# A planner's table of durations and hand-over times is replaced, and the first pair's product is placed behind the scores of all four first pairs

## The chip, the cores and the metric

The kernel runs on one core of one Trainium2 chip. The metric is the device time of one launch in microseconds (us). The core has five instruction streams that run side by side and wait for each other by semaphores: TensorE (PE), VectorE (DVE), ScalarE (ACT), GpSimd (POOL) and SyncE (SP), from which nearly all DMAs are issued.

## The reference

Windowed attention over 8 batches and 8 heads (576 tokens, 64 wide) is followed by a gated MLP over all 4608 tokens. Four heads see the last 32 positions, four see every fourth of the last 128.

```python
scores = scale * np.matmul(q, k.transpose(0, 1, 3, 2))
scores = np.where(masks[None, :, :, :], scores, -1000000000.0)
scores = scores - np.max(scores, axis=-1, keepdims=True)
attn = np.exp(scores)
attn = attn / (np.sum(attn, axis=-1, keepdims=True) + 1e-09)
out = np.matmul(attn, v)                       # (8, 8, 576, 64)
x = out.transpose(0, 2, 1, 3).reshape(4608, 512)
h = x @ w_in                                   # 512 -> 2048
g = h * (1.0 / (1.0 + np.exp(-1.702 * h)))
result = g @ w_out                             # 2048 -> 512
```

## The kernel before

Each f32 operand of the MLP is held as a high part, rounded to the matmul's input format, and a low part, the remainder, and a product is three matmuls (high by high, low by high, high by low).

**Attention** is made for pairs of heads. There are 32 pairs, four for each batch; pair k has number k % 4 in batch k // 4. A pair's scores (`scores`, L463) go to the PSUM tile `sp`. The softmax (`softmax`, L514) takes the row maximum (L502), subtracts it (L349), exponentiates on ACT (L506), sums (L520), adds 1e-9 to the sum (L510), inverts it (L512), and multiplies twice, once for each head (L349, on POOL or DVE). Then the weights are transposed by 32 x 32 blocks into `ct` (L529 for the first batch, L533 else). The first batch (pairs 0 to 3) is done by `first_attention` (L682) and `first_product` (L559), which writes the PSUM tile `first_x`. `drain_x` (L612) copies it on ACT into `xs` as the high part, and DVE subtracts to get the low part, also in `xs`; the last 64 tokens go to a rest. The four pairs give the four channels (128 rows each) of the first batch's tokens.

**The MLP** runs for batch 0, 1 and 2 as a `Group` (L817): for each of 16 units f, 12 large matmuls make `hp_m` (L848), ACT makes a tanh (L856), DVE the gating (L857), ACT and DVE split the result into `gh` and `gl`, and 12 more large matmuls add to `acc_m` (L785, L786, L789). Unit 1 of the first group uses the bank `sp`, unit 2 the bank `av`, all others the one bank `hp`. The batches after that run as three `Block`s of two with a scheme of seven products in place of eight (`up_p`, `up_q`, `up_r` at L991, `second_*` at L1106).

**Weights** come as f64 bit patterns and are decoded on the chip by `decode` (L355): n even is a `w_in` unit, n odd a `w_out` unit. A decode is a DMA (L384), two word operations on ACT (L394, L395), the sign on ACT (L388) or DVE (L390), a shift on DVE (L398), two pair operations on DVE, one of which POOL can take (L349), and a copy to the high part on ACT or DVE (L342, L344). They run during the first group, each ahead of the unit that needs it.

**The order.** The kernel does not write its order by hand. Every piece of work is given to `Plan.add` (L58) with its costs by engine (a negative cost on DVE marks one that shares a port with POOL), an urgency, a function that issues it, and the names it reads and writes. `Plan.placed` (L111) then runs a model of the five engines: it puts each piece on the engine where it would end first, in the order of the modelled times, taking the most urgent of those that can start. `LATENCY` (L45) is the model's time between the end of a piece and the start of a piece on another engine that needs it. `fetched` (L134) models that PE's instructions arrive in pieces of 256, with edges at 193 + 256 j. Where PE would be idle early on, `ordered` puts in filler matmuls: large ones (`idle<-ident`) or small ones (`idle<-ones`). After 130 us of the model's time it is redone three times with due times (`latest`, L80). The engines then run their lists strictly in this order. So a changed number can move any instruction of the program.

## Time and profile before

| | |
|---|---|
| median of 3 runs | 829.24 us (827.79 to 829.8) |
| the profiled execution's own time | 828.89 us |
| span of its trace | 827.2 us |
| mean granted clock of PE | 0.991 |
| HBM read and written | 140.64 and 45.09 MB |
| DMA, mean over the span | 227 GB/s |

The span is the time from the first to the last instruction in the trace; the rest of the execution's own time lies around it. In the profile, PE is the matmuls and PEld the weight loads that overlap them. A row such as `PE hp_m L848 <- DVE xs L349: 0.4, 1, 0.4` says that PE waited before line 848, which writes `hp_m`, 0.4 us in total, once, 0.4 us at the longest, for DVE's line 349 writing `xs`; where nothing in the profile released an engine, "issue" stands there. In a timeline, a row has the start, the busy time, engine, line, operation, output and inputs, and how many instructions it merges. A large matmul's busy time, about 0.39 us, overlaps the next one's.

### The profile page before, as it was taken

What the parts mean: (1) busy time and instruction counts of PE and PEld (TensorE: products, weight loads), DVE (VectorE), ACT (ScalarE), POOL (GpSimd) and SP (SyncE); (2) the same over time, 40 slices, a digit from 0 to 9 for tenths busy, and PEclk for the clock granted to TensorE, in tenths of its full rate; (3) what the DMA queues carried; (4) which work ended last, traced back from release to release, by engine and by line L of the source; (5) the groups of instructions that cost most, each with busy time, mean ns of one, the idle gap of its engine ahead of it and who ended that gap; (6) DMA issues with size and microseconds to landing.
All of it is one profiled execution on the core that took longest, in us unless ns stands there. A gap on an engine that the chain in (4) does not pass through costs nothing.

```text
span 827.2 us, 18837 instructions
## 1 busy us (share of the span) xinstructions
PE 811.2 (98%) x7240; PEld 653.5 (79%) x7240; DVE 669.7 (81%) x1104; ACT 515.0 (62%) x992; POOL 327.8 (40%) x296
## 2 busy tenths in 40 slices
PE   7899999999999999999999999999999999999997
PEld 4678777888878888878788788888888888888886
DVE  6898989787888778898989998977679876867575
ACT  7998986676676777586776655446446544544340
POOL 3343336566655663324235357331125431112251
PEclk8799999999999999999999999999999999999999
DMA  9476658889757567868878878675665658664546
GB/s 359 152 244 193 181 192 287 295 281 314 249 189 254 183 200 257 267 190 280 279 229 261 261 233 260 219 269 168 214 193 182 211 186 273 203 222 149 189 151 181
DMA packets 109610, 188.12 MB, mean 227 GB/s; under 512 B 26448, under 2 KB 55376, under 8 KB 109520
## 3 DMA queue, kind: packets, MB, share of 16 engines
q1 hardware_dynamic: 109376, 186.78, 69.3%
q8 instruction: 57, 0.93, 0.5%
q14 instruction: 33, 0.27, 0.1%
q10 hardware_dynamic: 144, 0.13, 0.0%
HBM read 140.64 MB, written 45.09 MB: 225 GB/s over the span
## 4 chain that ended last, share of the span: by engine, by line
PE 88%; DVE 7%; ACT 1%; issue 1%; DMA 1%; SPq 0%; DVEq 0%; ACTq 0%
PE hp_m L848 15%; PE up_q L991 9%; PE up_r L991 9%; PE up_p L991 8%; PE second_q_Q L1106 5%; PE second_r_Q L1106 5%; PE second_p_Q L1106 5%; PE acc_m L785 5%; PE acc_m L789 5%; PE acc_m L786 4%; PE sp L482 3%; PE second_r_Z L1106 3%; PE second_R L1106 3%; PE second_q_Z L1106 3%; PE second_p_Z L1106 2%; PE av L607 2%
## 5 line engine op out<-in xcount | busy, mean ns | idle before, releaser
L349 POOL TENSOR_TENSOR arena<-arena 128x256 f32<-128x256 f32 (+3 forms) x109 | 118.0, 1091 | 155.7 <-DVE wi_last_units L349 34.7
L848 PE MATMUL hp_m<-xs,wi_kept 128*128 128x512 f32 x504 | 129.1, 398 | 0.7 <-DVE xs L349 0.4
L848 PEld LDWEIGHTS hp_m<-xs,wi_kept 128*128 128x128 f32 x504 | 93.3, 188 | 22.5 <-DVE arena L857 1.6
L342 ACT ACTIVATE wo_kept<-arena 128x512 fp32r<-128x512 f32 x115 | 71.9, 629 | 42.3 <-PE second_r_Q L1106 11.4
L349 POOL TENSOR_TENSOR wo_kept<-arena,wo_kept 128x512 fp32r<-128x512 f32 x34 | 45.3, 1340 | 105.5 <-ACT wo_kept L342 72.2
L991 PE MATMUL up_p<-wi_kept,xs 128*128 128x512 f32 x336 | 84.7, 394 | 2.2 <-DVE arena L349 1.3
L991 PE MATMUL up_r<-wi_kept,xs 128*128 128x512 f32 x336 | 85.3, 389 | 0.0
L991 PE MATMUL up_q<-wi_kept,xs 128*128 128x512 f32 x336 | 83.4, 389 | 0.0
L991 PEld LDWEIGHTS up_p<-wi_kept,xs 128*128 128x128 f32 x336 | 62.1, 188 | 16.8 <-DVE arena L349 2.2
L991 PEld LDWEIGHTS up_q<-wi_kept,xs 128*128 128x128 f32 x336 | 63.0, 188 | 13.4 <-DVE arena L1013 0.3
L991 PEld LDWEIGHTS up_r<-wi_kept,xs 128*128 128x128 f32 x336 | 63.1, 188 | 13.1
L349 DVE TENSOR_TENSOR wo_kept<-arena,wo_kept 128x512 fp32r<-128x512 f32 x87 | 65.3, 761 | 5.9 <-ACT wo_kept L342 5.4
L349 POOL TENSOR_TENSOR wo_kept<-wi_last_units,wo_kept 128x512 fp32r<-128x512 f32 x23 | 31.9, 1388 | 84.6 <-ACT wo_kept L342 84.6
L785 PE MATMUL acc_m<-gh,wo_kept 128*128 128x512 f32 x156 | 61.7, 395 | 0.4 <-ACT arena L342 0.3
L786 PE MATMUL acc_m<-gh,wo_kept 128*128 128x512 f32 x156 | 60.9, 390 | 0.0
L349 POOL TENSOR_TENSOR pr<-pr,sm 128x320 f32<-128x320 f32 x52 | 43.3, 850 | 43.0 <-DVE sm L512 29.3
L342 ACT ACTIVATE bt<-ct 32x256 f32<-32x256 f32 (+1 forms) x127 | 55.2, 435 | 3.2 <-DVE ct L533 0.9
L1012 ACT ACTIVATE arena<-arena 128x512 f32<-128x512 f32 x60 | 37.5, 628 | 28.9 <-DVE arena L349 25.1
L349 DVE TENSOR_TENSOR gl<-arena,gh 128x512 fp32r<-128x512 f32 x53 | 44.9, 847 | 9.1 <-PE acc_m L789 6.4
L349 DVE TENSOR_TENSOR arena<-arena 128x512 f32<-128x512 f32 (+1 forms) x68 | 50.4, 747 | 0.4
L1013 DVE SCALAR_TENSOR_TENSOR arena<-arena 128x512 f32<-128x512 f32 x60 | 48.1, 807 | 0.7 <-ACT arena L1012 0.2
L342 ACT ACTIVATE wo_kept<-wi_last_units 128x512 fp32r<-128x512 f32 x47 | 29.6, 629 | 30.0 <-PE second_r_Z L1106 8.9
(261 smaller groups left out, 1826.6 us busy)
## 6 DMA issues: line engine op xcount, KB each, us to landing
xs<-sums SPq DMA_DIRECT2D x168, 256.0 KB, 3.3
out_weights<-sums_o SPq DMA_DIRECT2D x63, 512.0 KB, 3.8
qk<-qk_dram SPq DMA_DIRECT2D x29, 576.0 KB, 5.2
xs<-sums_o SPq DMA_DIRECT2D x21, 512.0 KB, 3.6
v<-vp_dram SPq DMA_DIRECT2D x28, 320.0 KB, 4.4
sums<-arena SPq DMA_DIRECT2D x32, 256.0 KB, 3.6
sums_o<-arena SPq DMA_DIRECT2D x32, 256.0 KB, 3.4
arena<-wi_dram SPq DMA_DIRECT2D x15, 512.0 KB, 4.7
```

The lines of the kernel that those rows point to most:

```text
L342: A.activation(dst, src, AF.Copy, scale=scale)
L349: (V if e == DVE else G).tensor_tensor(out=dst, in0=a, in1=b, op=op)
L482: T.matmul(dst[:, w:w + n], u["qk"][rows, at:at + 32], u["qk"][rows, S + first:S + first + n], start=not masked(k), stop=True, tile_positi ...
L607: T.matmul(u["x"][i][rows, at:at + last - first], u["v"][keys, a, m], bt[keys, m, a, first:last], start=(bank_, a) not in begun, stop=True ...
L785: T.matmul(self.acc[j], w[:, 0, cols], high, start=f == 0, stop=False)
L786: T.matmul(self.acc[j], w[:, 1, cols], high, start=False, stop=False)
L789: T.matmul(self.acc[j], w[:, 0, P * j:P * j + P], low, start=False, stop=f == NF - 1)
L848: T.matmul(hps[f], wi(f)[:, st, cols], mv[:, c], start=c == 0 and k == 0, stop=c == NC - 1 and k == 2)
L991: T.matmul(self.banks[place], xs[:, slot, at:at + P], wi_kept[:, 2 * a + c, mv], start=fresh and c == 0 and k == 0, stop=c == 1 and k == 2 ...
L1012: add({ACT: 0.60}, -10.0, lambda e: A.activation(unit(tmp), src(), AF.Tanh, scale=0.851), need, own(tmp))
L1013: add({DVE: -0.70 if need[0][0] == "A" else 0.70}, -10.0, lambda e: V.scalar_tensor_tensor(out=unit(dst), in0=unit(tmp), scalar=1.0, in1=s ...
L1106: T.matmul(self.second[key], w[:, st, cols], mv, start=fresh and y == 0 and k == 0, stop=y == 1 and k == 2, skip_group_check=True)
```

## The change

It has five parts.

1. **Hand-over times.** `LATENCY` goes from 0.2 or 0.3 us to 0.04 to 0.09 for the compute engines. A new table `FROM` keeps 0.2 and 0.3 for some ways (from PE, and after a DMA). `LEAVES` lets the model's engine take its next piece 0.045 to 0.10 us before the last one ends.
2. **Durations.** Several costs are changed, and an early instruction piece is taken to arrive 4.2 us after the edge before it where that edge is crossed before 6 us.
3. **The 1e-9** may be added on ACT.
4. **The first product.** `first_attention` no longer makes the product. It is made by the new `first_multiplied`, which reads a name that the fourth pair's scores write; the transposes, split off as `first_transposed`, stand ahead of it for pairs 0 and 1 and behind the product of the pair two ahead for pairs 2 and 3. Each product writes a name of its own (`four`), which `drain_x` reads.
5. **Zeros.** The zeroing of `bt` on POOL has urgency 44 in place of 20.

```diff
-LATENCY = {PE: 0.3, ACT: 0.2, DVE: 0.2, POOL: 0.2, DMA: 0.2}
+LATENCY = {PE: 0.06, ACT: 0.04, DVE: 0.04, POOL: 0.09, DMA: 0.2}
+FROM = {PE: {ACT: 0.2, DVE: 0.2}, DMA: {PE: 0.3, ACT: 0.2, DVE: 0.2, POOL: 0.2}}
+LEAVES = {PE: 0.0, ACT: 0.10, DVE: 0.085, POOL: 0.045, DMA: 0.0}
...
-                blocks.append(at + (6.1 if at < 18.0 else 4.2))
+                blocks.append(at + (4.2 if at < 6.0 else 6.1 if at < 18.0 else 4.2))
...
+            leaves = when + cost - min(LEAVES[e], 0.6 * cost)
             if e == POOL or (e == DVE and ops[i][0][e] < 0):
-                port[0] = when + cost
-
-            free[e] = when + (cost if e != DMA else 0.7 if cost < 100 else 0.43)
+                port[0] = leaves
+
+            free[e] = leaves if e != DMA else when + (0.7 if cost < 100 else 0.43)
...
-                    gap = 0.0 if to == e == PE else 0.13 if to == e else LATENCY[to]
+                    gap = 0.0 if to == e == PE else FROM.get(e, {}).get(to, LATENCY[to])
...
-        add({DVE: -0.75, ACT: 1.37}, urgency, take_sign, (R,), (R + "l",))
+        add({DVE: -0.65, ACT: 1.22}, urgency, take_sign, (R,), (R + "l",))
...
-        add({DVE: -0.15}, urgency, lambda e: V.tensor_scalar(
-            out=sm, in0=sm, scalar1=1.0e-9, scalar2=None, op0=ALU.add), (), (SM,))
+        def shift(e):
+            if e == ACT:
+                A.activation(sm, sm, AF.Copy, bias=1.0e-9)
+            else:
+                V.tensor_scalar(out=sm, in0=sm, scalar1=1.0e-9, scalar2=None, op0=ALU.add)
+
+        add({ACT: 0.2, DVE: -0.15}, urgency, shift, (), (SM,))
...
-            add({POOL: 0.85, DVE: -0.48}, urgency, lambda e, a=a: pair(
+            add({POOL: 0.73, DVE: -0.48}, urgency, lambda e, a=a: pair(
...
-            costs = {DMA: 82} if k < FIRST * NC else {ACT: 0.49, DVE: -0.33}
+            costs = {DMA: 82} if k < FIRST * NC else {ACT: 0.45, DVE: -0.29}
...
+            four = f"four{turn(k)}"
...
-                    e, part(xh[:, c]), src()), FOUR, (f"xh{c}.{n}",))
+                    e, part(xh[:, c]), src()), (four, *FOUR), (f"xh{c}.{n}",))
...
-    def first_attention(k, urgency):
+    def first_attention(k):
+
 
         load_qk(k)
         load_v(k)
-        add({PE: 1.5 if k else 2.3}, urgency - 1.0e5, lambda e: scores(k), (lots(k)[0],), ("sp",), count=180)
-        softmax(k, urgency)
-        add({PE: 1.4}, urgency - 1.0e5, lambda e: first_product(k), (lots(k)[1], f"ct{turn(k)}.0", f"ct{turn(k)}.1"), FOUR,
-            count=184)
-        drain_x(k, urgency)
+        add({PE: 1.5 if k else 2.3}, k - 1.0e5, lambda e: scores(k), (lots(k)[0],), ("sp", f"scores{k}"), count=180)
+        softmax(k, k)
+
+    def first_transposed(k):
+        y = turn(k)
+        pr, ct = prs[y], cts[y].rearrange("p h t a q -> p (h t a q)").rearrange("p (a n) -> p a n", a=2)
+        for a in range(2):
+            add({DVE: 0.50}, k, lambda e, a=a: V.transpose(
+                out=ct[:, a, 0:QT * W], in_=pr[:, a].rearrange("p t w -> p (t w)")), (f"pr{y}", f"pr{y}.{a}"), (f"ct{y}.{a}",))
+
+    def first_multiplied(k):
+
+
+        y = turn(k)
+        add({PE: 1.4}, k - 1.0e5, lambda e: first_product(k), (lots(k)[1], f"ct{y}.0", f"ct{y}.1", f"scores{NC - 1}"),
+            (f"four{y}",), count=184)
+        drain_x(k, k)
...
     for c in range(NC):
-        first_attention(c, c)
+        first_attention(c)
+        if c < 2:
+            first_transposed(c)
         if c in (1, 2):
             decode(c - 1, c + 1.3)
+    for c in range(NC):
+        first_multiplied(c)
+        if c < 2:
+            first_transposed(c + 2)
...
-            add({POOL: 1.2}, 20.0, lambda e: G.memset(bt, 0.0), (), ("bt", "btl", *zeroed))
+            add({POOL: 1.2}, 44.0, lambda e: G.memset(bt, 0.0), (), ("bt", "btl", *zeroed))
```

Lines in the changed kernel are shifted by up to 24. What the change does to the order is seen at three places.

On PE, right behind the first pair's scores (`sp_187`), there stood seven large fillers before; the first rows are:

```order
L482 MATMUL sp_187<-qk_126 32x64 x3
L482 MATMUL sp_187<-qk_126 32x48
L482 MATMUL sp_187<-qk_126 32x16
L1237 LDWEIGHTS ident
L1237 MATMUL idle<-ident 128x512
```

and now 19 small ones, behind which the second pair's scores (`sp_262`) begin:

```order
L487 MATMUL sp_187<-qk_126 32x64 x3
L487 MATMUL sp_187<-qk_126 32x48
L487 MATMUL sp_187<-qk_126 32x16
L1265 MATMUL idle<-ones 32x16 x19
L475 LDWEIGHTS ident
L475 MATMUL sp_262<-plain,ident 128x320
```

The seven large fillers are gone from there. Of the 30 large fillers of the program 13 are left, eight ahead of the third pair's scores and five ahead of the fourth's.

On PE, the fourth pair's scores (`sp_439`) were followed by the second pair's product and the first large matmuls of unit 0:

```order
L482 MATMUL sp_439<-arena 32x64 x3
L482 MATMUL sp_439<-arena 32x48
L482 MATMUL sp_439<-arena 32x16
L575 MATMUL first_x<-ct_92,arena 64x32 x6
L575 MATMUL first_x<-ct_92,arena 64x64 x24
L575 MATMUL first_x<-ct_92,arena 64x48 x8
L575 MATMUL first_x<-ct_92,arena 64x16 x8
L848 MATMUL hp_m_0_556<-xs,wi_kept 128x512 x3
```

Now (`sp_401`) the first pair's product stands there, and the other three come behind it:

```order
L487 MATMUL sp_401<-arena 32x64 x3
L487 MATMUL sp_401<-arena 32x48
L487 MATMUL sp_401<-arena 32x16
L580 MATMUL first_x<-ct_91,v_129 64x32 x6
L580 MATMUL first_x<-ct_91,v_129 64x64 x24
L580 MATMUL first_x<-ct_91,v_129 64x48 x8
L580 MATMUL first_x<-ct_91,v_129 64x16 x8
L580 MATMUL first_x<-ct_92,arena 64x32 x6
```

The first pair's product has moved from behind the third scores to behind the fourth. The large matmuls have moved from among the products to behind the last of the four, with no filler between: nine of unit 0 (channels 0 to 2), three of unit 1, three of unit 0 (channel 3), nine of unit 1, six of unit 2, and then the first `acc_m`.

On ACT, from the tanh of unit 0 to that of unit 1, stood these rows (L394, L395 and L388 are decode's word operations and sign, L342 copies to a high part):

```order
L856 ACTIVATE arena<-hp_m_0_556 128x512
L394 ACTIVATE arena<-arena 128x512
L395 ACTIVATE arena<-arena 128x512
L342 ACTIVATE wi_kept<-arena 128x512
L342 ACTIVATE gh_73<-arena 128x512
L388 ACTIVATE arena<-arena 128x512
L856 ACTIVATE arena<-hp_m_1_623 128x512
```

and now these, L399, L400, L393 and L347 being the same four operations:

```order
L874 ACTIVATE arena<-hp_m_0_678 128x512
L399 ACTIVATE arena<-arena 128x512
L393 ACTIVATE arena<-arena 128x512
L347 ACTIVATE gh_73<-arena 128x512
L347 ACTIVATE wi_kept<-arena 128x512
L400 ACTIVATE arena<-arena 128x512
L874 ACTIVATE arena<-hp_m_1_697 128x512
```

A sign now stands ahead of the copy to `gh_73`. From the tanh of unit 0 to that of unit 10 ACT has 101 instructions in place of 84 (14 signs in place of 10), and DVE, between the same units' gatings, 101 in place of 90. In the whole program POOL has 259 in place of 296, ACT 1033 in place of 992, and 31 of the 32 additions of 1e-9 are on ACT.

More of the change, by code (lines that the diff above doesn't have):

```diff
@@ L522, in softmax @@
         for a in range(2):
-            add({POOL: 0.85, DVE: -0.48}, urgency, lambda e, a=a: pair(
+            add({POOL: 0.73, DVE: -0.48}, urgency, lambda e, a=a: pair(
                 e, pr[:, a], pr[:, a], sm[:, a, :, None].broadcast_to([P, QT, W]), ALU.mult), (SM,), (f"{PR}.{a}",))
         if k < NC:
-            for a in range(2):
-                to = ct.rearrange("p h t a q -> p (h t a q)")[:, a * QT * W:a * QT * W + QT * W]
-                add({DVE: 0.48}, urgency, lambda e, a=a, to=to: V.transpose(
-                    out=to, in_=pr[:, a].rearrange("p t w -> p (t w)")), (PR, f"{PR}.{a}"), (f"{CT}.{a}",))
             return
         for half in (0, 1):
-            add({DVE: 0.42}, urgency, lambda e, half=half: V.transpose(
+            add({DVE: 0.50}, urgency, lambda e, half=half: V.transpose(
                 out=ct[:, half].rearrange("p t a q -> p a t q"), in_=pr[:, :, :, 32 - 32 * half:64 - 32 * half]),
@@ L649, in drain_x @@
                 add({ACT: 0.12 + size * (0.0019 if dilated(k) else 0.00094)}, urgency, lambda e, part=part, src=src: copy(
-                    e, part(xh[:, c]), src()), FOUR, (f"xh{c}.{n}",))
+                    e, part(xh[:, c]), src()), (four, *FOUR), (f"xh{c}.{n}",))
                 add({DVE: 0.08 + size / (490 if dilated(k) else 820)}, urgency, lambda e, part=part, src=src: pair(
-                    e, part(xl[:, c]), src(), part(f32(xh[:, c])), ALU.subtract), (*FOUR, f"xh{c}.{n}"), (f"xl{c}.{n}",))
+                    e, part(xl[:, c]), src(), part(f32(xh[:, c])), ALU.subtract), (four, *FOUR, f"xh{c}.{n}"), (f"xl{c}.{n}",))
             for n, (part, src) in enumerate(rests):
                 add({ACT: 0.22, DVE: 0.2}, urgency, lambda e, part=part, src=src: copy(
-                    e, part(rests_x[:, 1, c]), src()), FOUR, (f"xr1{c}.{n}",))
+                    e, part(rests_x[:, 1, c]), src()), (four, *FOUR), (f"xr1{c}.{n}",))
             store_rest(b, c, urgency)
```

## The prediction

> **What bounds the kernel now.** I read the page's busy shares first, then busy time by stretch of the span, then the list of waits, then the timeline where the waits stand.
>
> ```profile
> span 827.2 us, 18837 instructions
> PE 811.2 (98%) x7240; PEld 653.5 (79%) x7240; DVE 669.7 (81%) x1104; ACT 515.0 (62%) x992; POOL 327.8 (40%) x296
> PEclk8799999999999999999999999999999999999999
> ```
> ```profile
> 15.00:20.00 5.00, 3.75 (x118) 2.26 (x118) 3.81 (x10) 4.52 (x8) 2.81 (x4) 0.63 1.04 412
> 20.00:25.00 5.00, 3.19 (x139) 2.46 (x137) 4.56 (x12) 5.00 (x8) 2.66 (x3) 0.50 0.46 179
> 25.00:30.00 5.00, 4.30 (x84) 2.54 (x86) 4.90 (x9) 4.26 (x8) 2.71 (x4) 0.51 0.64 201
> 30.00:35.00 5.00, 5.00 (x158) 3.83 (x141) 3.32 (x9) 4.31 (x6) 1.38 (x2) 1.00 0.05 17
> 500.00:600.00 100.00, 100.00 (x442) 82.55 (x441) 78.12 (x114) 49.72 (x85) 34.54 (x25) 1.00 0.69 223
> ```
> ```profile
> PE sp L482 <- issue: 3.4, 2, 1.8
> PE first_x L575 <- issue: 0.9, 1, 0.9
> PE up_p L991 <- DVE arena L349: 1.3, 2, 0.7
> PE up_p L991 <- DVE arena L1013: 0.9, 1, 0.9
> ```
>
> The columns of a stretch are its length, then busy time and count of PE, weight load, DVE, ACT and POOL, the granted clock, DMA share and GB/s. TensorE is the bound: 98% busy, and between 500 and 600 us it makes 442 large matmuls in 100.0 us, 0.226 us each. Nothing in the change alters how many such matmuls there are. So time comes from two places only: how early the large matmuls can run without a break, and what PE waits for after that. The second is small: the up_p waits, 1.3 + 0.9 = 2.2 us, are most of it. The first is the start: from 15 to 30 us PE is busy 11.2 of 15 us, at half its clock, partly with filler, and three stops without a releaser ("issue") cost 4.3 us.
>
> **The change, part by part.** All sums are made against the profiled execution, 828.89 us, of which 1.7 us lie outside the span and are left as they are. The median of the three runs is 829.24, 0.35 us above.
>
> *The stops.* The rows of PE around them:
>
> ```profile
> 5.07 1.44 PE L482 MATMUL sp<-qk 64*32 64x64 f32 x84 [0.15 <-DMA qk<-qk_dram]
> 6.44 3.14 PE L1237 MATMUL idle<-ident 128*128 128x512 bf16 x7
> 10.79 2.12 PE L1237 MATMUL idle<-ident 128*128 128x512 bf16 x9
> 16.02 0.40 PE L482 MATMUL sp<-arena 64*32 64x64 f32 x21 [1.76 <-issue]
> 22.31 1.37 PE L482 MATMUL sp<-arena 64*32 64x64 f32 x75 [1.60 <-issue]
> 25.70 0.91 PE L575 MATMUL first_x<-ct,arena 32*64 32x64 f32 x39 [0.90 <-issue]
> 26.54 1.65 PE L848 MATMUL hp_m<-xs,wi_kept 128*128 128x512 f32 x3
> 38.18 3.92 PE L848 MATMUL hp_m<-xs,wi_kept 128*128 128x512 f32 x16 [0.43 <-DVE xs L349]
> ```
>
> Each stop sits where the planner's formula puts an edge of a 256-instruction piece (193 + 256 j), and the releases lie 6.3 us (16.02 to 22.31) and 3.4 us (to 25.70) apart: reaching one edge starts the fetch of the next piece, slow while the DMA share is about 1.0. In the changed order 19 small fillers carry PE over edge 449 right behind the first scores, at 6.5 + 0.6 = 7.1 us, where before it was crossed in the second scores, near 10.1. The piece behind it should be there by 7.1 + 6.1 = 13.2 (6.1 is the middle of 5.9, from 10.1 to 16.02, and 6.3), before the third scores reach edge 705 at about 14.5: no stop. The fourth scores then stop at edge 961 until 14.5 + 6.1 = 20.6 and end at 21.2, where before they ended at 22.31 + 1.37 = 23.7. Gain 2.5 us.
>
> *The fourth pair.* Its softmax is what the first unbroken matmuls end up waiting for:
>
> ```profile
> 23.72 0.82 DVE L502 TENSOR_REDUCE mx<-sp 128x10 f32<-128x640 f32 x1 [0.37 <-PE sp L482]
> 24.89 0.78 DVE L349 TENSOR_TENSOR pr<-sp,mx 128x640 f32<-128x640 f32 x1
> 25.76 0.74 ACT L506 ACTIVATE pr<-pr 128x640 f32<-128x640 f32 x1 [0.29 <-DVE pr L349]
> 26.58 0.81 DVE L520 TENSOR_REDUCE sm<-pr 128x10 f32<-128x640 f32 x1
> 28.12 1.20 DVE L510 TENSOR_SCALAR sm<-sm 128x10 f32<-128x10 f32 x1
> 29.35 0.22 DVE L512 RECIPROCAL sm<-sm 128x10 f32<-128x10 f32 x1
> 29.65 1.73 POOL L349 TENSOR_TENSOR pr<-pr,sm 128x320 f32<-128x320 f32 x2 [0.36 <-DVE sm L512]
> 33.31 0.51 DVE L529 STREAM_TRANSPOSE ct<-pr 128x320 f32<-128x320 f32 x1
> 34.00 1.08 PE L575 MATMUL first_x<-ct,arena 32*64 32x64 f32 x80
> 35.11 1.09 ACT L342 ACTIVATE xs<-first_x 128x512 fp32r<-128x512 f32 x1
> 37.04 1.09 DVE L349 TENSOR_TENSOR xs<-first_x,xs 128x512 fp32r<-128x512 f32 x1
> ```
>
> Reduce to the end of the transpose took 33.82 - 23.72 = 10.1 us, though its steps sum to 6.8; the rest stood behind other work. I walk the new rows with these durations. The maximum waits for two word shifts and an ISA ahead of it on DVE: 21.6 to 22.4; subtraction to 23.2. The exponential stands on ACT behind one L388 and the first channel's copies, so it starts near 23.9 and ends at 24.7; sum to 25.6; shift on ACT (priced at 0.23, the nearest row being a 64-wide copy of that length) to 25.9; reciprocal to 26.2; POOL to 27.7; second transpose to 28.5. That is 7.3 us from scores to transpose. The DVE shift took 1.20 us here for ten elements; that goes. The fourth product follows at 28.6 and ends at 29.8. The third channel's copy on ACT, queued behind two L388, ends near 30.9 and its subtraction near 31.9; the fourth's copy at 32.3, its subtraction at 33.4 instead of 38.1.
>
> *The measure of the start* is the time of a large matmul less 0.226 us for each one done before it. Before: 20 were done by 38.18 (from the row at 26.54 to the one at 36.94), 38.18 - 20 x 0.226 = 33.6. Now 14 stand ahead (nine of unit 0, three of unit 1, two of the fourth channel): 33.4 - 14 x 0.226 = 30.2. **Gain 3.4 us**, at full clock.
>
> *What is late next.* By the same walk the first tanh runs at 34.5 and gh is written at 37.3, while PE reaches the first acc at 30.2 + 30 x 0.226 = 37.0: a wait of 0.3. After that ACT is the question.
>
> ```profile
> 38.88:96.47 57.59, 57.59 (x604) 45.98 (x603) 53.02 (x92) 51.31 (x85) 21.65 (x18) 1.00 0.72 224
> ```
> ```profile
> L388 ACT ACTIVATE arena<-arena 128x512 f16<-128x512 f32 x10 | 13.7, 1373 | 0.0
> L394 ACT ACTIVATE arena<-arena 128x512 f32<-128x512 f32 x18 | 11.9, 670 | 1.1 <-DVE wo_kept L349 0.7 <-POOL wi_kept L349 0.4
> L856 ACT ACTIVATE arena<-hp_m 128x512 f32<-128x512 f32 x10 | 6.0, 599 | 4.4 <-PE hp_m L848 4.2
> ```
> ```profile
> 71.42 0.30 PE L607 MATMUL av<-bt,v 64*64 64x96 f32 x2
> 72.37 0.96 PE L789 MATMUL acc_m<-gl,wo_kept 128*128 128x512 f32 x3
> 96.47 0.60 ACT L856 ACTIVATE arena<-hp_m 128x512 f32<-128x512 f32 x1 [0.69 <-PE hp_m L848]
> ```
>
> From the tanh of unit 0 to that of unit 10 (38.88 to 96.47) ACT was busy 51.3 of 57.6 us with 84 instructions, and 4.2 us of its idle time were waits for PE. In the new order 101 stand there: four more L388, seven more word steps (L394, L395), two more casts, one exponential, four shifts. With the spacing of back-to-back rows (1.1 for an L388, about 0.55 else, their tails overlapping) that adds 10.6 us: 61.9. From 34.5 the tanh of unit 10 comes at 96.4, while PE, 3.1 us ahead, has its input by 93.3. The lag that costs nothing is what stands on PE before the bank is used again, 12 acc matmuls (2.7) and one product (71.42 to 72.37, 0.95), less tanh and gating (0.60 + 0.69) and two hand-overs: 2.2. **Loss 0.9 us**; none if ACT runs ahead, 3.0 if it also idles the 2.1 us that it idled for others than PE.
>
> *The rest.* POOL loses 37 instructions, mostly 512-wide ones that DVE takes at about 0.68 us; 31 small shifts leave DVE. DVE goes from 670 to some 687 us, 83%, hidden by its idle time; were that gone, it would be up to 17 us. On PE the last attention product stands in the third of the first block's eight steps, before in the seventh, so the up_p stage shares DVE with less softmax. I credit a third of the 2.2 us, **0.7 us**; bounds: all 2.2 gained, or as much lost. The zeroing of bt (L1207) still stands ahead of the fourth pair's POOL work, but ends before the reciprocal: nothing; 0.3 to 0.9 if POOL runs late. On SP one weight load goes past one first_v load, whose matmuls come at 28.6: nothing, as both queue before 14 us.
>
> Sum: 828.9 - 3.4 + 0.3 + 0.9 - 0.7 = **826.0**.
>
> [...] The clock was granted in halves: 0.50 from about 16 to 30 us, 1.00 again after a dense stretch of large matmuls (26.5 to 29.5). At half clock filler takes 3.14 / 7 = 0.45 us, at full 2.12 / 9 = 0.235. The change drops 17 of the 30 large fillers, all seven behind the first scores among them. [...]
>
> **Rivals.**
> *The clock stays low.* For: no fillers between 7.1 and 9.1 us nor behind the fourth scores. The eight fillers ahead of the third scores then take 3.4 us, which moves that chain about 1.0 us; the late restart costs 0.7 more at the first large matmuls (0.48 instead of 0.226 each, by the row at 26.54), mostly under waits. [...] Against: eight fillers in a row may be enough to open it.
> *The fetch does not come earlier.* The piece released at 22.31 came just as DMA emptied (share 1.04 to 20 us, 0.46 after). If the queue, not the request, sets its time, the fourth scores end at 22.9; the gain of 3.4 halves and ACT leaves 0.5: 827.7.
> *ACT becomes the bound, slower than before.* Place: tanh of unit 0 to unit 10. If ACT keeps its idle share of before, 6.3 of 57.6, the stretch is 61.9 / 0.89 = 69.5 us, and the tanh of unit 10 comes at 104.0 instead of 96.5; less the 2.2 free, PE is 5.3 us behind the kernel before, and without the later credit that gives 834.2. It decides when ACT idles over 2.2 us there. For: DVE is 92% busy there and hands ACT its input. Against: most of that idle time was waiting for PE.
>
> **How the numbers follow.** Forecast 0.45, clock 0.24, fetch 0.14, ACT 0.17. A change of 0.3%, 2.5 us, is about what a measurement of this kernel can tell from none: the forecast counts as faster (0.45), clock and fetch as the same (0.38), ACT as slower (0.17). Low end: no loss on ACT and all later waits gone, 826.0 - 0.9 - 1.5 = 823.6, with 0.6 for the walk's error, 823.0. High end: 831.0, which takes in both "same" rivals and ACT idling half of 6.3 us or somewhat more; the upper part of that rival is left out.
>
> **What would show it.** Right: no "issue" stop in the second and third scores; fourth scores ended by about 21; the fourth subtraction into xs ended near 33.4 and 14 large matmuls ahead; tanh of unit 10 before 96.5. Wrong: granted clock 0.5 past 30 us; a stop beyond 21; PE waits for ACT or DVE between 37 and 95 us of over 2 us in all; new PE waits after 130 us.

## The result and the profile after

| | before | after |
|---|---|---|
| median | 828.93 us (5 runs, 827.79 to 829.8) | 857.65 us (5 runs, 856.66 to 859.91) |
| ratio after / before | | 1.0352, 95% interval 1.0333 to 1.0371 |
| span of the profiled execution | 827.2 us | 854.9 us |

The changed kernel is slower by 28.7 us, where 826.0 us had been forecast with a range up to 831.0. The page of the changed kernel, busy times and granted clock by slice:

```profile
span 854.9 us, 18873 instructions
PE 812.5 (95%) x7261; PEld 652.4 (76%) x7261; DVE 685.0 (80%) x1100; ACT 523.8 (61%) x1033; POOL 281.2 (33%) x259
PEclk9599999999999999999999999999999999999999
```

PE is as long busy as before (811.2); its idle time went from 827.2 - 811.2 = 16.0 to 42.4 us. The work is the same, the waits are new. The waits of PE in the changed kernel (total, times, longest):

```profile
PE hp_m L866 <- DVE arena L875: 12.0, 16, 2.1
PE first_x L580 <- ACT xs L347: 5.0, 1, 5.0
PE second_p_Q L1124 <- DVE arena L1145: 2.6, 2, 2.1
PE acc_m L803 <- ACT arena L347: 2.2, 2, 1.1
```

The first row is the gating (L857 before): sixteen times a unit's product found its bank not yet read. Before, this row had 0.2 us. Where the idle time lies is read from stretches cut at marks. From the first tanh to the last one of the third group, in the kernel before:

```profile
38.88:339.26 300.38, 299.57 (x3685) 240.31 (x3684) 255.38 (x448) 225.29 (x470) 152.17 (x152) 1.00 0.74 239
```

and in the changed one, with the stretch from the tanh of unit 0 to that of unit 10 and one later stretch:

```profile
41.24:104.00 62.76, 60.65 (x629) 47.87 (x631) 59.43 (x102) 60.95 (x102) 24.76 (x19) 1.00 0.71 225
...
41.24:371.75 330.51, 314.61 (x4180) 246.56 (x4181) 282.35 (x480) 255.87 (x561) 165.72 (x163) 1.00 0.72 231
...
500.00:600.00 100.00, 96.63 (x422) 78.36 (x421) 85.59 (x123) 47.89 (x82) 26.68 (x19) 1.00 0.69 221
```

In the three groups PE idled 0.8 us before and 15.9 after, which is more than half of the loss; between 500 and 600 us, where it idled nothing, 3.4. PE is also busy 15 us longer in the groups, largely with attention that the new order makes earlier. The tanh of unit 10 comes 7.5 us later than before (104.0 for 96.47), and up to it both kernels had made the same 132 matmuls of `hp_m`: so some 20 of the 28 us are lost behind it.

**The start** of the changed kernel, first PE with what reads `first_x` (the row at 27.16 is the fourth pair's exponential), then the stretches of 5 us:

```profile
17.66 0.95 PE L487 MATMUL sp<-arena 64*32 64x64 f32 x70
20.10 0.48 PE L487 MATMUL sp<-arena 64*32 64x48 f32 x14 [1.49 <-issue]
24.27 1.40 PE L580 MATMUL first_x<-ct,arena 32*64 32x64 f32 x71 [1.71 <-issue]
25.70 0.66 ACT L347 ACTIVATE xs<-first_x 128x432 fp32r<-128x432 f32 x2 [1.76 <-PE first_x L580]
27.16 0.73 ACT L511 ACTIVATE pr<-pr 128x640 f32<-128x640 f32 x1
30.98 0.90 DVE L699 STREAM_TRANSPOSE ct<-pr 128x320 f32<-128x320 f32 x2
32.97 1.08 ACT L347 ACTIVATE xs<-first_x 128x512 fp32r<-128x512 f32 x1
34.10 1.47 PE L580 MATMUL first_x<-ct,arena 32*64 32x64 f32 x80 [5.04 <-ACT xs L347]
36.87 1.07 DVE L354 TENSOR_TENSOR xs<-first_x,xs 128x512 fp32r<-128x512 f32 x1
38.04 1.09 ACT L347 ACTIVATE xs<-first_x 128x512 fp32r<-128x512 f32 x1 [3.56 <-DVE xs L354]
39.28 1.12 DVE L354 TENSOR_TENSOR xs<-first_x,xs 128x512 fp32r<-128x512 f32 x1 [1.34 <-ACT arena L347]
```
```profile
20.00:25.00 5.00, 3.19 (x175) 3.02 (x179) 4.39 (x7) 3.74 (x6) 3.71 (x4) 0.50 0.79 293
25.00:30.00 5.00, 2.14 (x120) 1.93 (x113) 2.43 (x5) 3.62 (x10) 1.78 (x3) 0.50 0.34 113
30.00:35.00 5.00, 0.90 (x61) 0.90 (x65) 2.81 (x7) 4.48 (x8) 1.56 (x3) 0.50 0.00 0
35.00:40.00 5.00, 5.00 (x54) 4.05 (x42) 2.57 (x4) 1.96 (x4) 1.07 (x2) 0.52 0.37 112
```

The fourth scores ended at 20.6, a little before the forecast 21.2. The second product stopped at an instruction piece until 24.27, and the copies of the first pair, whose own product was done by then, started only when the second one had ended (25.67). The fourth pair's exponential stands behind these copies on ACT: it began at 27.16. The fourth product did not follow its transposes (ended at 31.88) but the ACT copy of the third product (ended at 34.05), and from there copy and subtraction take turns: the fourth copy waits for the third subtraction. The last subtraction ends at 40.40 in place of the forecast 33.4. And the clock stays at 0.50 until about 40 us.

**A wait in a group**, from DVE, POOL, ACT and PE around 253 us of the changed kernel:

```profile
250.24 0.69 DVE L354 TENSOR_TENSOR xs<-arena,xs 128x512 fp32r<-128x512 f32 x1 [0.65 <-ACT xs L347]
250.95 0.69 DVE L354 TENSOR_TENSOR gl<-arena,gh 128x512 fp32r<-128x512 f32 x1
251.04 1.75 POOL L354 TENSOR_TENSOR arena<-wo_last 128x512 f32<-128x512 f32 x1 [0.85 <-DMA sums_o<-arena]
251.56 2.93 DVE L354 TENSOR_TENSOR xs<-arena,xs 128x512 fp32r<-128x512 f32 x2
252.09 0.59 ACT L874 ACTIVATE arena<-hp_m 128x512 f32<-128x512 f32 x1
252.76 3.70 POOL L354 TENSOR_TENSOR arena<-arena 128x256 f32<-128x256 f32 x4
254.41 0.67 DVE L875 SCALAR_TENSOR_TENSOR arena<-arena,hp_m 128x512 f32<-128x512 f32 x1
255.14 0.96 PE L866 MATMUL hp_m<-xs,wi_kept 128*128 128x512 f32 x3 [1.50 <-DVE arena L875]
```

The tanh ended at 252.68. The gating stood on DVE behind two subtractions that took 2.93 us together beside POOL's work (the same operation took 0.69 at 250.24, before POOL began), so it began 1.7 us late and PE waited 1.50. The plan had priced each of the two at 0.61 less 0.085. The hand-over itself is as the new table has it: the gating ended at 255.08 and PE began at 255.14, 0.06 us later.

### The profile page after: what moved, and what is told of

Read it like the earlier page. It is cut to its first block, busy times and chain, and to the rows that moved or that the text cites. A ratio compares the mean times of both kernels' runs of the same rounds, so it can differ in the third digit from the quotient of the medians.

```text
span 854.9 us, 18873 instructions
## 1 busy us (share of the span) xinstructions
PE 812.5 (95%) x7261; PEld 652.4 (76%) x7261; DVE 685.0 (80%) x1100; ACT 523.8 (61%) x1033; POOL 281.2 (33%) x259
## 4 chain that ended last, share of the span: by engine, by line
PE 53%; DVE 18%; ACT 16%; issue 6%; DMA 4%; SPq 1%; POOL 1%; DVEq 0%; ACTq 0%; POOLq 0%
PE up_r L1009 9%; PE up_q L1009 7%; PE up_p L1009 7%; PE second_q_Q L1124 5%; ACT bt L347 5%; PE second_r_Q L1124 4%; PE second_p_Q L1124 4%; DVE arena L354 3%; PE second_q_Z L1124 3%; PE second_R L1124 3%; PE hp_m L866 2%; ACT arena L347 2%; PE second_r_Z L1124 2%; PE second_p_Z L1124 2%; DVE pr L354 2%
## 5 line engine op out<-in xcount | busy, mean ns | idle before, releaser
L354 POOL TENSOR_TENSOR arena<-arena 128x256 f32<-128x256 f32 (+3 forms) x97 | 101.3, 1050 | 138.5 <-DVE wi_last_units L354 62.4
L866 PE MATMUL hp_m<-xs,wi_kept 128*128 128x512 f32 x504 | 133.6, 404 | 10.4 <-DVE arena L875 10.0
L347 ACT ACTIVATE wo_kept<-arena 128x512 fp32r<-128x512 f32 x112 | 70.0, 630 | 51.5 <-PE second_r_Q L1124 8.2
L1009 PE MATMUL up_p<-wi_kept,xs 128*128 128x512 f32 x336 | 82.6, 391 | 1.0 <-DMA xs<-sums 0.8
L354 DVE TENSOR_TENSOR wo_kept<-arena,wo_kept 128x512 fp32r<-128x512 f32 x99 | 72.5, 745 | 9.8 <-ACT wo_kept L347 8.6
L354 POOL TENSOR_TENSOR wo_kept<-arena,wo_kept 128x512 fp32r<-128x512 f32 x22 | 28.9, 1317 | 116.9 <-ACT wo_kept L347 78.2
L347 ACT ACTIVATE bt<-ct 32x256 f32<-32x256 f32 (+1 forms) x127 | 55.5, 437 | 15.3 <-DVE ct L538 9.4
L354 DVE TENSOR_TENSOR arena<-arena 128x512 f32<-128x512 f32 (+1 forms) x76 | 58.8, 779 | 3.6 <-ACT arena L347 2.5
L1031 DVE SCALAR_TENSOR_TENSOR arena<-arena 128x512 f32<-128x512 f32 x60 | 45.1, 756 | 9.9 <-ACT arena L1030 9.5
L354 DVE TENSOR_TENSOR wo_kept<-wi_last_units,wo_kept 128x512 fp32r<-128x512 f32 x42 | 29.9, 713 | 25.6 <-ACT wo_kept L347 24.2
L347 ACT ACTIVATE gh<-arena 128x512 fp32r<-128x512 f32 x59 | 37.4, 634 | 16.2 <-DVE arena L875 4.7
```

The lines of the kernel that those rows point to most:

```text
L347: A.activation(dst, src, AF.Copy, scale=scale)
L354: (V if e == DVE else G).tensor_tensor(out=dst, in0=a, in1=b, op=op)
L866: T.matmul(hps[f], wi(f)[:, st, cols], mv[:, c], start=c == 0 and k == 0, stop=c == NC - 1 and k == 2)
L1009: T.matmul(self.banks[place], xs[:, slot, at:at + P], wi_kept[:, 2 * a + c, mv], start=fresh and c == 0 and k == 0, stop=c == 1 and k == 2 ...
L1031: add({DVE: -0.70 if need[0][0] == "A" else 0.70}, -10.0, lambda e: V.scalar_tensor_tensor(out=unit(dst), in0=unit(tmp), scalar=1.0, in1=s ...
```

## The experiments

For each run there is a second number beside the time: the **plan's sum**, the cost less LEAVES of all pieces that the planner put on an engine, added up by running the planner alone, over the busy time of that engine in the trace. This sum takes LEAVES off every piece, also off one behind which the engine of the model idles. Counted as the trace is, by busy time, the changed kernel's plan has 640 us on DVE and 497 on ACT, so it is 7% and 5% short rather than 12% and 13%; e13_scaled has 702 and 555 by this count, e12_stays 673 on DVE, and where pieces leave when they end the two ways agree. The last column is the total wait of `hp_m` for the gating and its count.

| run | us | ratio to before, 95% interval | DVE plan / trace | ACT plan / trace | gating wait |
|---|---|---|---|---|---|
| before | 828.9 | | 677 / 670 | 558 / 515 | 0.2, 1 |
| after | 857.7 | 1.0333 to 1.0371 | 604 / 685 | 458 / 524 | 12.0, 16 |
| e1_hand | 849.5 | 1.0234 to 1.0268 | 614 / 694 | 460 / 516 | 9.5, 15 |
| e2_nohand | 830.6 | 1.0012 to 1.0031 | 673 / 667 | 556 / 523 | none |
| e3_first | 841.2 | 1.0120 to 1.0172 | 686 / 678 | 556 / 516 | 1.4, 1 |
| e4_shift | 828.1 | 0.9983 to 1.0006 | 680 / 668 | 558 / 515 | 0.7, 1 |
| e5_leaves | 842.5 | 1.0140 to 1.0182 | 603 / 694 | 458 / 515 | 3.5, 6 |
| e6_gaps | 836.7 | 1.0071 to 1.0101 | 691 / 700 | 549 / 508 | 3.2, 4 |
| e7_short | 851.6 | 1.0252 to 1.0288 | 628 / 694 | 481 / 516 | 8.2, 11 |
| e8_margin | 855.6 | 1.0299 to 1.0334 | 609 / 683 | 458 / 523 | 10.3, 14 |
| e9_dve0 | 849.1 | 1.0228 to 1.0268 | 672 / 678 | 462 / 529 | 7.8, 9 |
| e10_act0 | 846.2 | 1.0188 to 1.0222 | 622 / 706 | 535 / 506 | 6.0, 11 |
| e11_told | 834.9 | 1.0055 to 1.0091 | 678 / 677 | 551 / 517 | 1.9, 1 |
| e12_stays | 838.4 | 1.0104 to 1.0134 | 705 / 666 | 563 / 517 | none |
| e13_scaled | 835.9 | 1.0065 to 1.0095 | 678 / 682 | 522 / 524 | 2.5, 4 |
| e14_scaled_down | 843.2 | 1.0154 to 1.0185 | 606 / 689 | 491 / 517 | 8.2, 12 |
| e15_neutral | 832.2 | 1.0027 to 1.0055 | 678 / 676 | 557 / 513 | none |
| e16_noleaves | 841.1 | 1.0127 to 1.0161 | 685 / 687 | 553 / 521 | 2.5, 6 |
| e17_banks | 858.8 | 1.0337 to 1.0367 | 604 / 686 | 458 / 524 | 12.5, 18 |
| e18_nohand_banks | 829.8 | 0.9992 to 1.0013 | 673 / 666 | 556 / 523 | 0.4, 1 |

### Which part of the change

Part 1 alone, on the kernel before:

```diff
-LATENCY = {PE: 0.3, ACT: 0.2, DVE: 0.2, POOL: 0.2, DMA: 0.2}
+LATENCY = {PE: 0.06, ACT: 0.04, DVE: 0.04, POOL: 0.09, DMA: 0.2}
+FROM = {PE: {ACT: 0.2, DVE: 0.2}, DMA: {PE: 0.3, ACT: 0.2, DVE: 0.2, POOL: 0.2}}
+LEAVES = {PE: 0.0, ACT: 0.10, DVE: 0.085, POOL: 0.045, DMA: 0.0}
...
```

> The kernel before with part 1 alone (LATENCY, FROM, LEAVES and the gap rule). Theory H (the hand-over times let the modelled chip run ahead of the real one, so that orders are taken in which the gating and the tanh come late): most of the 25 us that were lost after 41 us come back, 845 to 856 us; PE waits of hp_m for the gating in groups 0 to 2 of over 10 us in all, tanh of the last unit of group 2 late by 20 us or more; the start as before, within 1 us. Theory S (the 1e-9 on ACT): 826 to 832 us. Theory C (any new order scatters the time by some us either way): 824 to 838 us, waits at other places than in the changed kernel.

It lost 20.7 us. Its row answers the first wait of the changed kernel, a little under theory H's mark of 10 us:

```profile
PE hp_m L851 <- DVE arena L860: 9.5, 15, 1.3
```

The last tanh of the third group came at 358.3 (339.3 before), 19 us late (20 expected). The start was not as before: the first tanh came at 42.1, where 38.9 within 1 us was expected.

Parts 2 to 5 without part 1:

```diff
-LATENCY = {PE: 0.06, ACT: 0.04, DVE: 0.04, POOL: 0.09, DMA: 0.2}
+LATENCY = {PE: 0.3, ACT: 0.2, DVE: 0.2, POOL: 0.2, DMA: 0.2}
...
-            free[e] = leaves if e != DMA else when + (0.7 if cost < 100 else 0.43)
+            free[e] = when + (cost if e != DMA else 0.7 if cost < 100 else 0.43)
...
```

> The changed kernel with the hand-over times of before (parts 2 to 5 only). Theory H: the loss at the start stays (3 to 5 us), the later one goes: 830 to 836 us, and no PE wait for the gating of over 2 us in all after 45 us. Theory S, or the changed durations: 850 us or more, as the changed kernel. Theory C: 832 to 845 us.

830.6 us: all but 1.8 us of the loss went with part 1, and no product waited for a gating. The start was still late, but less: the last subtraction ended at 38.97 and the first tanh ran at 40.4, against 40.40 and 41.2 in the changed kernel, and the clock was 0.74 from 35 to 40 us, not 0.52.

Part 4 alone, with the fetch of before:

```diff
...
-        first_attention(c, c)
+        first_attention(c)
+        if c < 2:
+            first_transposed(c)
...
+    for c in range(NC):
+        first_multiplied(c)
+        if c < 2:
+            first_transposed(c + 2)
```

> The kernel before with part 4 alone (order of the first four pairs, products behind all scores). Theory F (the four products share one PSUM tile, first_x, so the third and fourth product wait for drains of others, while the new names no longer tell the planner so): the fourth product starts over 1.5 us after its transposes, the last subtraction into xs ends at 38 to 41 us, the measure of the start is 2 to 5 us later than the 33.6 of before, and the time is 831 to 835 us, since nothing after it is touched. If instead part 4 is good and its loss in the changed kernel came from the hand-over times: 825 to 829 us.

841.2, outside of what any theory said. The last subtraction ended at 40.53, and the start was late as expected; but some 8 us more were lost behind it, at waits of several kinds of 1 to 3 us. Since the same order of the first pairs cost only 1.8 us in e2_nohand, this is taken to be a price of the order that came out with it and not of part 4; no run tells the two apart.

Part 3 alone:

```diff
...
-        add({DVE: -0.15}, urgency, lambda e: V.tensor_scalar(
-            out=sm, in0=sm, scalar1=1.0e-9, scalar2=None, op0=ALU.add), (), (SM,))
...
+        add({ACT: 0.2, DVE: -0.15}, urgency, shift, (), (SM,))
```

> The kernel before with part 3 alone (1e-9 may be added on ACT). Theory S (the sum goes through the queue of ACT, two more hand-overs for each pair, so that the softmax is late and DVE waits): 838 us or more, with DVE waits for ACT's shift of over 5 us in all. Theory H: 826 to 832 us.

828.1, the same as before: theory S fell.

### Which half of part 1, and why

LEAVES alone, and LATENCY with FROM and the gap rule alone, each on the kernel before:

```diff
+LEAVES = {PE: 0.0, ACT: 0.10, DVE: 0.085, POOL: 0.045, DMA: 0.0}
...
+            leaves = when + cost - min(LEAVES[e], 0.6 * cost)
...
-            free[e] = when + (cost if e != DMA else 0.7 if cost < 100 else 0.43)
+            free[e] = leaves if e != DMA else when + (0.7 if cost < 100 else 0.43)
```

> The kernel before with LEAVES alone (an engine of the model takes its next piece 0.045 to 0.10 us before the last one ends; LATENCY and the gap rule as before). Part 1 alone cost 20.7 us; this splits it. Theory Q (LEAVES makes short instructions too short, so ACT and DVE run behind the order and the tanh and the gating come late): 840 to 850 us, tanh more than 0.8 us behind its product on the mean in groups 1 and 2. Theory G (the shorter gaps leave too little room in the chain product, tanh, gating, product): 826 to 833 us.

```diff
...
-                    gap = 0.0 if to == e == PE else 0.13 if to == e else LATENCY[to]
+                    gap = 0.0 if to == e == PE else FROM.get(e, {}).get(to, LATENCY[to])
```

> The kernel before with LATENCY, FROM and the gap rule alone (no LEAVES). Theory G: 840 to 850 us, the next product of PE under 0.4 us behind the gating on the mean in groups 1 and 2. Theory Q: 826 to 833 us. If both this and the other half lose about 10 us, the two add up and neither theory stands alone.

They lost 13.0 and 7.2 us, whose sum is about the 20.7 of both: neither stands alone, and LEAVES is the larger. In e5_leaves the tanh started 0.68 us behind the end of its product's last matmul on the mean of groups 1 and 2 (0.36 before): later, as theory Q has it, but under its mark of 0.8. Two repairs of the changed kernel:

```diff
-            leaves = when + cost - min(LEAVES[e], 0.6 * cost)
+            leaves = when + cost - (LEAVES[e] if cost > 0.47 else 0.0)
```

> The changed kernel in which LEAVES holds only for pieces that cost over 0.47 us, so that the copies into bt (chip: one each 0.44 to 0.46 us, in the changed model 0.35) and other short ones take their whole cost. Theory Q: 835 to 845 us, most of the later loss gone, the loss at the start kept. Theory G: 850 us or more.

```diff
-            add({ACT: 0.60}, -10.0, lambda e: A.activation(g32, hps[f], AF.Tanh, scale=0.851), (place,), ("g32",))
+            add({ACT: 0.60}, -10.0, lambda e: A.activation(g32, hps[f], AF.Tanh, scale=0.851), (place,), ("g32",), slack=0.2)
```

(the second with the same slack at the gating and at each unit's first matmuls)

> The changed kernel with 0.2 us of slack added, in the plan, ahead of each tanh, each gating and each unit's product in the three groups (nothing else has slack). Theory G or any theory by which only this chain is planned too tightly: 832 to 842 us, waits of hp_m for the gating under 3 us in all. Theory Q (the queues of ACT and DVE as a whole run behind the order): 845 to 858 us, the tanh as late behind its product as in the changed kernel.

851.6 and 855.6. Short pieces were 6 us of it, less than theory Q expected and in theory G's range. But slack in the chain itself, with all else as it was, gave back 2 us: theory G, that the chain product, tanh, gating is planned too tightly, fell. What is late, then, is the queue that the tanh and the gating stand in. So theory O: the plan's queues as a whole are shorter than the chip's. The table's sums say so for the changed kernel (DVE 604 planned, 685 us busy; ACT 458 and 524) and not for the one before. Undoing LEAVES on one engine at a time:

```diff
-LEAVES = {PE: 0.0, ACT: 0.10, DVE: 0.085, POOL: 0.045, DMA: 0.0}
+LEAVES = {PE: 0.0, ACT: 0.10, DVE: 0.0, POOL: 0.045, DMA: 0.0}
```

> The changed kernel with LEAVES of DVE at 0 (ACT 0.10 and POOL 0.045 stay). By the changed kernel's numbers the pieces that its plan puts on DVE (each cost less LEAVES) take 604 us and those on ACT 458; the trace has 685 and 524 us of busy time. In the kernel before the same sums are 677 and 558, the trace has 670 and 515. Theory O (LEAVES makes the modelled queues 12% too short, so that too much is put into the groups and onto DVE), with DVE as the engine that matters: 838 to 850 us, DVE busy near 670 us or POOL over 300. If ACT is the engine that matters: 852 us or more.

```diff
-LEAVES = {PE: 0.0, ACT: 0.10, DVE: 0.085, POOL: 0.045, DMA: 0.0}
+LEAVES = {PE: 0.0, ACT: 0.0, DVE: 0.085, POOL: 0.045, DMA: 0.0}
```

> The changed kernel with LEAVES of ACT at 0 (DVE 0.085 and POOL 0.045 stay). Theory O with ACT as the engine that matters: 838 to 850 us, the tanh under 0.8 us behind its product on the mean in groups 1 and 2. With DVE as that engine: 852 us or more. If both this and the run with DVE at 0 get back half, both queues matter alike.

849.1 and 846.2: they gave back 8.5 and 11.5 us, each within the range for its engine, so both queues matter about alike. The opposite of LEAVES on the kernel before:

```diff
+STAYS = {PE: 0.0, ACT: 0.0, DVE: 0.03, POOL: 0.03, DMA: 0.0}
...
-            free[e] = when + (cost if e != DMA else 0.7 if cost < 100 else 0.43)
+            free[e] = when + (cost + STAYS[e] if e != DMA else 0.7 if cost < 100 else 0.43)
```

> The kernel before with the opposite of LEAVES: DVE and POOL of the model stay 0.03 us longer with each piece. Theory O (what counts is whether the modelled queues are as long as the chip's; before they are 677 for 670 us on DVE): no loss, 826 to 831 us. Theory C (any new order scatters by several us either way): outside of that, as likely above as below.

838.4, against theory O's 826 to 831. But no product waited for a gating, and the groups ended 5 us earlier than before (last tanh at 334.2). The largest single piece of the loss is one wait behind them, PE's timeline at 353 us:

```profile
353.30 2.42 PE L608 MATMUL av<-bt,v 64*64 64x96 f32 x44 [4.84 <-ACT bt L343]
```

with the clock at 0.70 in the 15 us around it. So there are two things: what the groups do, and what any new order may run into. The next four are to tell them apart. All costs of ACT, DVE and POOL in the changed kernel times 1.12, which makes its plan's sums those of the chip, with LEAVES and the new gaps left in:

```diff
+        costs = {e: c * (1.12 if e in (ACT, DVE, POOL) else 1.0) for e, c in costs.items()}
```

> The changed kernel with every cost on ACT, DVE and POOL in the plan times 1.12, which makes its sums (cost less LEAVES) about as long as the busy times of its trace; hand-over times and LEAVES as changed. Theory O (the modelled queues are too short): 832 to 845 us, the product over 0.6 us behind the gating on the mean in groups 1 and 2, against 0.37 in the changed kernel. Theory G (the hand-over times as such): 850 us or more, product under 0.5 us behind. Theory C (scatter of any new order): anywhere, the gap behind the gating unrelated to it.

and in the kernel before:

```diff
+        costs = {e: c * (0.88 if e in (ACT, DVE, POOL) else 1.0) for e, c in costs.items()}
```

> The kernel before with every cost on ACT, DVE and POOL in the plan times 0.88; hand-over times as before, no LEAVES. Theory O: 840 us or more, the product under 0.55 us behind the gating in groups 1 and 2 (0.79 before), and waits of hp_m for the gating of over 3 us. Theory G: under 836 us.

835.9 and 843.2: with the right sums 21.7 of the 28.7 us came back although every hand-over time of the change stayed, and with sums that are too short, by 12% on DVE and 5% on ACT, the kernel before lost 14 us although no hand-over time was touched. The rows of the waits, in this order:

```profile
PE hp_m L867 <- DVE arena L876: 2.5, 4, 0.8
```
```profile
PE hp_m L849 <- DVE arena L858: 8.2, 12, 2.3
```

The other mark of theory O failed: the next product began, on the mean of groups 1 and 2, 0.43 us behind the end of the gating in e13_scaled (over 0.6 expected, 0.37 in the changed kernel) and 0.65 in e14_scaled_down (under 0.55 expected). The mean of that gap is not what decides, the few long waits are. One cost of no meaning, and the changed kernel without LEAVES:

```diff
-        add({ACT: 0.75}, urgency, lambda e: A.activation(prs[y], prs[y], AF.Exp, scale=0.125), (), (PR,))
+        add({ACT: 0.76}, urgency, lambda e: A.activation(prs[y], prs[y], AF.Exp, scale=0.125), (), (PR,))
```

> The kernel before with one cost moved by 0.01 us (the exponential, 0.75 to 0.76), which says nothing of the chip. Theory C: the order of most of the program changes, and the time by 3 to 12 us. Theory O alone: 827 to 831 us.

```diff
-LEAVES = {PE: 0.0, ACT: 0.10, DVE: 0.085, POOL: 0.045, DMA: 0.0}
+LEAVES = {PE: 0.0, ACT: 0.0, DVE: 0.0, POOL: 0.0, DMA: 0.0}
```

> The changed kernel without LEAVES, its LATENCY, FROM and gap rule kept. Theory O: 832 to 842 us, near the 836.7 us that the gaps alone made of the kernel before, and waits of hp_m for the gating of under 4 us. Theory G: 848 us or more.

832.2: a hundredth of a microsecond in one cost moves the time by 3 us (0.27 to 0.55%). That is the scatter of theory C, smaller than what LEAVES does. 841.1 without LEAVES: 16.5 us came back, inside theory O's range; the rest may be the start (first tanh at 43.1) and the gaps.

The table as a whole says more than any one order. In nine versions the plan's sum is well below the trace on DVE or on ACT (after, e1_hand, e5_leaves, e7_short, e8_margin, e9_dve0, e10_act0, e14_scaled_down, e17_banks): they took 842.5 to 858.8 us, with 3.5 to 12.5 us of waits for the gating. The ten other versions took 828.1 to 841.2, with at most 3.2. The two sets do not overlap, though they come close, and both are spread by some 13 to 16 us.

### The start

Each first product names both halves of `first_x` as written, on e2_nohand:

```diff
-            (f"four{y}",), count=184)
+            ("four0", "four1"), count=184)
```

> The changed kernel with the hand-over times of before (830.6 us) in which each of the first products names both halves of first_x as written, so that the plan knows that the third and fourth product wait for the drains of the ones before, as the chip's order does. Theory F (that unknown wait costs at the start): last subtraction into xs before 37 us in place of 38.97, the fourth product within 1 us of its transposes or its drain in the plan's order, and 827.5 to 829.5 us. If the wait is not what costs: 830 us or more.

834.9, and the last subtraction at 39.09: worse. The plan made another order with more filler, so this says nothing on the wait. The next two keep the order and change the tile:

```diff
-    first_x = four.__enter__().tile([P, NC, GT], F32, tag="x", name="first_x")
+    quads = four.__enter__()
+    first_x = [quads.tile([P, GT], F32, tag=f"x{g}", name=f"first_x{g}") for g in range(NC)]
...
```

> The changed kernel, its plan untouched, with first_x as four tiles of one bank each, so that the columns of two pairs no longer lie inside one another's range; the copies and subtractions that read all four are issued as three or four each. Theory F (the fourth product waits for the copy of the third one, 34.10 us where its transposes ended at 31.88, though they share no element): the fourth product starts by 32.6 us, the last subtraction into xs ends 1 to 2 us earlier than 40.4, and the time is 1 to 2 us under the changed kernel's, 855 to 857 us. If that wait was for something else: 34 us again, and no gain.

> The same four tiles in the changed kernel with the hand-over times of before (830.6 us; its third and fourth product at 30.02 and 33.29 us, last subtraction ended at 38.97). Theory F: the fourth product by 32.3 us, the last subtraction by 37.8, and 828.5 to 830 us, no better than the kernel before beyond what a measurement can tell. If the start decides nothing any more, because ACT and DVE are the later ones up to unit 10: 830 to 831 us.

Rows of the two runs, copy or product and last subtraction:

```profile
32.75 1.14 ACT L348 ACTIVATE xs<-first_x 128x128 fp32r<-128x128 f32 x4
33.26 2.00 PE L581 MATMUL first_x<-ct,arena 32*64 32x64 f32 x80 [4.09 <-ACT xs L348]
38.38 1.27 DVE L355 TENSOR_TENSOR xs<-first_x,xs 128x128 fp32r<-128x128 f32 x4 [0.79 <-ACT arena L348]
```
```profile
30.37 1.64 PE L580 MATMUL first_x<-ct,arena 32*64 32x64 f32 x80
...
34.42 1.27 DVE L354 TENSOR_TENSOR xs<-first_x,xs 128x128 fp32r<-128x128 f32 x4
```

In the changed kernel the product now starts while the copy of the third is still running (33.26, where 32.6 was expected and the four copies end at 33.89), but it still waits for the first of them, although the two share no element and their columns no longer lie inside one another's range. What the pairs do share is all four tiles, so the wait goes by tile or by something coarser. The last subtraction ends 0.75 us earlier (1 to 2 expected), and the whole gained nothing (858.8; 855 to 857 expected). With the old hand-over times the fourth product comes 2.9 us earlier and the last subtraction ends 3.3 us earlier (35.69); the span is 826.0 in place of 828.0, the median 0.8 us lower, as theory F had it: a start 3.3 us earlier was worth 0.8 us here. So half of theory F holds: accesses to `first_x` by PE, ACT and DVE took turns (in the changed kernel copy to 34.05, product 34.10 to 35.57, subtraction 36.87 to 37.94, copy 38.04 to 39.13, subtraction from 39.28), that makes the start later, and it is not by the ranges of the columns. Whether the chip or the program asks for these turns no run shows. In the changed kernel itself the four tiles gave back 0.75 of the 7 us.

No version beats the kernel before by more than can be measured.

## Why the prediction was wrong, point by point

*The bound* was right: PE's work is the same, and only waits count.

*The stops and the fetch* were right: no stop in the second and third scores; the fourth ended at 20.6 (forecast 21.2). One stop beyond 21 was left, 1.71 us at 24.27. The fetches stand on the instruction queue, q8, as packets of 16 KB: in the kernel before they start at 13.5, 19.9 and 23.4 us, ahead of the ends of the stops at 16.02, 22.31 and 25.70, and in the changed one at 17.6 and 21.8, ahead of 20.10 and 24.27. The second of them started 3.9 us behind the end of the stop at 16.02, where the DMA share was 1.02 in between, and the third 1.05 us behind 22.31, where it was 0.26; but in the changed kernel it was 1.7 us behind 20.10 at a share of 1.01, so the share alone does not say how slow a fetch is.

*The fourth pair* was wrong by 7 us, and here is the first failed step: "The fourth product follows at 28.6 and ends at 29.8." The walk parts from the trace earlier: "The exponential stands on ACT behind one L388 and the first channel's copies, so it starts near 23.9". It began at 27.16, because those copies had waited for the second product, with its stop, until 25.70. The transposes ended at 31.88, not 28.5, behind the exponential and the second pair's subtraction; then the product waited for the third's copy until 34.10. The prediction took copies, subtractions and products of different pairs to run side by side because their names in the plan are separate; on the one tile `first_x` they took turns (a copy to 34.05, the product from 34.10). e18_nohand_banks shows that by itself: four tiles in its place, in the same order as e2_nohand, brought the fourth product 2.9 us earlier (30.37 for 33.29).

*The measure of the start*: 30 large matmuls were done by 44.44, so 44.44 - 30 x 0.226 = 37.7, where 30.2 was forecast and 33.6 was before. In place of a gain of 3.4 there is a loss of 4.1, of which the low clock is 2.15: the 30 took 44.44 - 35.51 = 8.93 us, 6.78 at full clock. The rival of the low clock was right in this and too small (0.7); its other half did not come: the eight fillers ahead of the third scores took 2.44 us and not 3.4 (three fillers at a clock of 0.50 took 1.46 us at 17.94 in the kernel before), and the clock fell to 0.50 only between 19.0 and 19.5 us (0.82 there). How late the clock restarts, on which that rival's time and chance rest, no run shows as a rule: it came back 4.3 us behind the first large matmuls of 35.51 here, and 3.0 to 3.5 us behind those of 26.54 in the kernel before (0.59 from 29.5 to 30.0 us, 1.00 after).

*ACT from unit 0 to unit 10* was right as a length: 61.9 us forecast, 62.76 measured with 60.95 busy. But it began at 41.24 and not at 34.5. The tanh of unit 10 at 104.0 is the very number of the ACT rival, reached in another way: that rival started at 34.5 and had ACT idle 7.6 us, while it idled 1.8. That the number agrees is luck.

*The later waits* are the failed step that decides: "I credit a third of the 2.2 us, 0.7 us; bounds: all 2.2 gained, or as much lost." They cost 20.2 us: 27.7 in the spans less the 7.5 at unit 10. The prediction compared the two orders by counts and took any order that the planner makes to be as good on the chip. It is so only as far as the plan's numbers are the chip's. The sum that would have shown it was at hand: the pieces on DVE take 604 us by the new table (cost less LEAVES), though the prediction itself had put DVE at 687 us; with that short a queue the plan puts more into the groups and fewer pieces on POOL (259 for 296), and the tanh and the gating stand behind more than fits. e13_scaled and e14_scaled_down show this from both sides, each with one order.

*Zeros* were not tried by themselves; in e2_nohand they cost nothing that shows. *The shift* on ACT costs nothing (e4_shift).

What stays open: how much of the 20 us is scatter. It was 3 us for e15_neutral, but e3_first lost 12 us, e12_stays 10 and e6_gaps 7 with plan's sums on DVE no more than 1% shorter than the chip's; whether the short gaps cost something of their own was not told apart from that. So e14_scaled_down's loss of 14 us is not far from what a new order alone may cost; its waits for the gating, 8.2 us, stand out more clearly.

Why the sums come out short can be read from plan and trace together. On DVE the durations of the changed kernel's 1100 instructions add up to 744.5 us in the trace, and 754 of them began before the one ahead had ended, by 0.079 us on the mean. The plan has 696 us of costs and lets every piece leave 0.085 us early: the overlap is about right for one hand-over, but the costs are too low. In the kernel before, 677 us of costs stood against 728.4 us of durations, with 58.7 us of overlap that the plan did not have: the two errors cancelled, and LEAVES took one of them away. A part of what the costs lack are rows of DVE beside POOL, such as the one at 251.56.

## What to carry to other kernels

A planner's table is one thing: the new hand-over times were nearer to the trace than the old ones (0.06 us at 255.14, 0.079 of overlap), and the plan that they made was worse, because the sums no longer fitted. Before changing such a table, add up what the plan gives each engine and set it beside the busy time of the trace; costs times 0.88 came with a loss of 14 us here, in one order. And an order of some 4000 pieces scatters by some us when one cost moves by 0.01, so a small gain is read from several such neighbours, not from one.

## What was not expected of the hardware

From 20 to 35 us the clock stayed at 0.50 while PE was 0.9 to 3.2 us of each 5 busy, and it came back only some 4.3 us after dense large matmuls began at 35.51 (0.50 up to 39.5, 0.70 from there to 40.0, then 1.00). What sets this time no run shows. Two DVE subtractions of 128x512 beside POOL's work took 2.93 us together, where one before it took 0.69; of the 275 DVE instructions of that size with two operands in SBUF that ran in the changed kernel with POOL at rest, none took over 0.73 us, and of the 82 that ran beside POOL for 30% of their time or more, 42 took over 1 us. That the two share a port, as the plan's negative costs have it, no run shows; these times are what was measured.
